# Rows of the maxima's matmuls in a projection stage, and three small operations moved from ScalarE to VectorE

## The chip, the cores and the metric

The kernel runs on one core of a Trainium2 chip. The metric is the device time of one execution in microseconds (us). The profile is that of one execution on the chip; its engines are PE (TensorE matmul), PEld (TensorE weight load), DVE (VectorE), ACT (ScalarE), POOL (GpSimd) and SP (SyncE, which here only issues DMAs).

## The reference

Both halves of the result read the same `x` (2048 rows of 448). `a` is a sliding, dilated local attention with 8 neighbours, `b` a full attention with 16 heads of 28 channels; a gate per row mixes the two.

```python
def _B_ref(x, wqkv, wo):
    B, S, D = x.shape              # 1, 2048, 448
    H = 16
    Dh = D // H                    # 28
    qkv = (lambda x, *d: x.transpose(*d))((x @ wqkv).reshape(B, S, 3, H, Dh), 2, 0, 3, 1, 4)
    q, k, v = qkv[0], qkv[1], qkv[2]
    scores = jnp.einsum("bhqd,bhkd->bhqk", q, k) * (Dh ** -0.5)
    p = _softmax(scores, axis=-1)
    o = jnp.einsum("bhqk,bhkd->bhqd", p, v)
    return (lambda x, *d: x.transpose(*d))(o, 0, 2, 1, 3).reshape(B, S, D) @ wo

x = A_x
g = _sigmoid((x * gate_w).sum(-1, keepdims=True))
a = _A_ref(x, A_wqkv, A_wo)        # 8 neighbours, 2 apart, own softmax
b = _B_ref(x, B_wqkv, B_wo)
return g * a + (1 - g) * b
```

## The kernel before, in words

The order of every engine is written out by hand: instructions run on each engine in the order in which the program issues them. There are three stages.

**Projections** (up to about 253 us of the profile). 92 tiles of `x @ w` are made, each a sum of products of a high and a low part of the operands (`ORDER`). The first ten tiles use all 128 rows of the array (`project`, 11 products). From tile 10 on, `project_halves` splits the contraction in two (11 products in one half, 10 in the other): half 0 uses rows 0 to 63 of the array, half 1 rows 64 to 127. Each half has a list (`todo[half]`), and the two lists are emitted in turn, one entry of each, so that neighbouring instructions use different halves and run beside each other; the two halves write the two banks of `PJ[n % 2]`. 28 tiles are of the kind "qk" (moving operand of 512 columns, line L303), the other 64 of the kinds "v" and "a" (448 or 450 columns, line L308).

Into 80 of these tiles, 11 to 90, work of the next stage is woven: the softmax of `b` needs the maximum of every row of the scores, and a first, rough product (28 channels, high parts alone) is made for it (`s1_mm`), four a tile, two PSUM tiles `PM[0]` and `PM[1]` of two banks each, and each `PM` is read by one VectorE maximum over 1024 columns (`TENSOR_REDUCE MX<-r`). One head has 28 channels at rows 32h to 32h+27. In the projections the product takes the whole half of 64 rows: the queries lie in two tiles, `QP[..][0]` for even heads and `QP[..][1]` for odd ones, and the rows of the other head of the half are zero. `s1_half(k, half)` is one such product; it is an entry of the half's list at index 2 (k = 0) and index 9 (k = 1), so both halves make one at the same place, and the second of the two issues the maximum.

**Attention** (`scores`, 253 to 827 us): 16 units (four groups of four heads, four blocks of 512 queries) of 16 steps. A step makes twelve products of 28 or 30 rows, four beside each other in the array, two exponentials on ScalarE, the products `av` with the values (`do_av`, 128 rows by 32 columns), and up to three more maxima's products, until all 1024 of them are made at step 235. At a unit's end `fin_copy` copies `av` out of its one PSUM bank, and `fin_hi` and others normalise and round it; hooks put each at a step. The last 21 steps have none.

**Output** (from 827 us): 16 tiles of the last projection.

Of the kernel before, what the change touches and what calls it, by code (L numbers as in the profile page):

```python
# [10 lines left out]
AF = mybir.ActivationFunctionType  # L11
ALU = mybir.AluOpType
X = mybir.AxisListType.X
ET = mybir.EngineType

S, D, H, DH = 2048, 448, 16, 28
# [4 lines left out]
NU = NG * NB  # L21
NMX = 192
# [3 lines left out]
def gated_mix_kernel(ctx: ExitStack, tc: tile.TileContext, xT, xn, gw, wA, wB, woAB, out):  # L26
    nc = tc.nc
# [25 lines left out]
    PJ, PM = PS[0:2], PS[2:4]  # L53
# [19 lines left out]
    MX = cp.tile([128, NMX], F32, name="MX")  # L73
# [13 lines left out]
    half = {}  # L87
# [10 lines left out]
    def dma_r(dst, src):  # L98
        nc.sync.dma_start(dst.bitcast(F32), src.bitcast(F32))
# [7 lines left out]
    def load_part(u, name, src):  # L107
        g, b = divmod(u, NB)
        t = sp.tile([128, 512], F32R, name=name)
        for h in range(4):  # L110
            r = 112 * g + DH * h
            dma_r(t[32 * h:32 * h + DH, :], src[r:r + DH, 512 * b:512 * b + 512])
        return t

    Qs = {}

    def load_q(u):
        Qs[u] = load_part(u, "QH", qk_hi), load_part(u, "QL", qk_lo)
        for i in range(2):
            dma_r(Qs[u][0][DH + i::32, :], nm[u][16 * i:16 * i + 16, :].rearrange("(h q) c -> h (q c)", h=4))  # L120

# [3 lines left out]
    s1c = [0]  # L125
    s1e = 64 * NU
    finished = []

    def load_qhi(u):
        g, b = divmod(u, NB)  # L130
        qhis[u] = QP[u % 2]
        for h in range(4):
            r = 112 * g + DH * h
            dma_r(qhis[u][h % 2][32 * h:32 * h + DH, :], qk_hi[r:r + DH, 512 * b:512 * b + 512])

    def s1_mm(n, bank, half=False):
        u, i = divmod(n, 64)
        qs, kc, h = i // 16, i // 4 % 4, i % 4
        if u == 0:
            qs, kc = i // 8 % 4, 2 * (i // 32) + i // 4 % 2  # L140
        if i == 0 and u + 1 < NU:
            load_qhi(u + 1)
        r = slice(64 * (h // 2), 64 * (h // 2) + 64) if half else slice(32 * h, 32 * h + DH)
        nc.tensor.matmul(bank, qhis[u][h % 2][r, 128 * qs:128 * qs + 128],  # L144
                         KH[u // NB % 3][r, 512 * kc:512 * kc + 512], start=True, stop=True)

# [9 lines left out]
        s1c[0] = n + k  # L156


    def s1_half(k, half):
        n = s1c[0]  # L160
        s1_mm(n + k + 2 * half, PM[k][:, half, :], True)
        halves[k] += 1
        if halves[k] == 2:
            halves[k] = 0
            m = MX[:, n % NMX:n % NMX + 4].rearrange("p (a b) -> p a b", b=2)[:, :, k]
            nc.vector.tensor_reduce(m, PM[k], axis=X, op=ALU.max)  # L166
            if k == 1:
                s1c[0] = n + 4
                if s1c[0] % 64 == 0:
                    finished.append(n // 64)  # L170

    halves = [0, 0]

# [18 lines left out]
    def max_turn(t):  # L194
        r = sp.tile([128, 32], F32, name="nms")
        nc.vector.transpose(r, t.bitcast(F32))
        return r
# [18 lines left out]
    with tc.tile_pool(name="xp", bufs=1) as xp, tc.tile_pool(name="wp", bufs=2) as wp:  # L216
# [99 lines left out]


        todo = [[], []]

        def project_halves(n, s1):  # L320
            if n % 2 == 0:
                for m in (n, n + 1):
                    low = (tiles[m][2] if tiles[m][1] == "qk" else tiles[m][-1] // 4) < 2
                    for half in range(2):
                        l = [p for p in ORDER if p != (0, 1, 3) or half == (0 if low else 1)]
                        l = [(m, product, (m, p, half, i == 0, i == len(l) - 1)) for i, p in enumerate(l)]
                        if s1[m - n]:
                            l[8:8] = [(m, s1_half, (1, half))]
                            l[2:2] = [(m, s1_half, (0, half))]
                        todo[half] += l  # L330
            while any(l and l[0][0] == n for l in todo):
                for l in todo:
                    if l:
                        _, f, x = l.pop(0)
                        f(*x)
# [83 lines left out]
        r, t = xst[:, 0, 0:3, :], xst[:, 0, 3, :]  # L419
# [5 lines left out]
        for kt in range(3):  # L425
            if kt < 2:
                nc.vector.tensor_copy(xh[0][:, kt, :], r[:, kt, :])
            nc.vector.tensor_tensor(out=xl[0][:, kt, :], in0=r[:, kt, :], in1=xh[0][:, kt, :].bitcast(F32),
                                    op=ALU.subtract)
        nc.vector.tensor_tensor(out=tail[64:128], in0=t[64:128], in1=tail[64:128].bitcast(F32), op=ALU.subtract)  # L430
        nc.vector.tensor_tensor(out=wl0[:, 3, 0:256], in0=wt0[:, 0:256], in1=wh0[:, 3, 0:256].bitcast(F32),
                                op=ALU.subtract)
# [27 lines left out]
        for n, t in enumerate(tiles):  # L460
# [4 lines left out]
            for w in splits:  # L465
                i, k = (n - splits[w][0]) * splits[w][1], splits[w][1]
# [36 lines left out]
            if parts and parts[0][0] <= n:  # L503
                _, u, t = parts.pop(0)
                max_store(u, max_turn(t))
            if finished and n < len(tiles) - 3:
                u = finished.pop(0)
# [12 lines left out]
            if n == 76:  # L520
                load_q(0)
# [5 lines left out]
    def at(pos, st, f):  # L527
        hooks.setdefault((st, pos), []).append(f)

    def run(pos, st):  # L530
        for f in hooks.pop((st, pos), ()):
            f()
# [8 lines left out]
    av = pool.tile([128, 512], F32, name="av")  # L541
# [33 lines left out]
    def mtile(name):  # L575
        return pm.tile([128, 512], F32, tag="M", name=name)
# [15 lines left out]
    for nme in ("k", "v"):  # L592
        for i in range(2):
            t = a1.tile([128, HALO + NJ, 56], F32, name=f"{nme}t{i}")
# [110 lines left out]
    for c in range(8):  # L705
# [20 lines left out]
        n = 0  # L726
# [17 lines left out]
    def issue(eng, st, limit):  # L744
        q = lists[eng]
        i = 0
        while i < min(len(q), LOOK):
            key, name, cost, needs, f = q[i]
            if any(d in names and issued.get(d, 10 ** 6) + lag > st for d, lag in needs):
                i += 1  # L750
                continue
            if eng in late:
                if late[eng] + cost > limit:
                    return
                late[eng] += cost
            f()
            issued[name] = st
            q.pop(i)
            i = 0
# [22 lines left out]
    def a_done(st):  # L782
        adone.append(st)
        assert st < OP0 + 24, st
        actx.close()
        oP["2"] = ctx.enter_context(tc.tile_pool(name="wop2", bufs=2))
        for k in range(4):
            at("end", max(st, OP0 + 23) + 2 * k, lambda k=k: (op_load_a(0, k), op_load_b(0, k)))
            at("dve", max(st, OP0 + 23) + 2 * k + 2, lambda k=k: op_split(0, k, nc.vector.tensor_copy))
# [61 lines left out]
    fin = {}  # L851
    def fin_copy(u):
        t = mp.tile([128, 512], F32, name="osb")
        nc.scalar.activation(t, av, AF.Copy)  # L854
        fin["o"] = t


# [26 lines left out]

    def fin_hi(u):
        fin["hi"] = mtile("onhi").bitcast(F32R)
        nc.scalar.activation(fin["hi"], fin["on"], AF.Copy)

    def fin_lo(u, eng):
        fin["lo"] = mtile("onlo").bitcast(F32R)  # L890
# [19 lines left out]
    for u in range(NU - 1):  # L910
        f = NJ * (u + 1)
        l = {NU - 3: (1, 2, 5, 6, 9, 12, 13, 15), NU - 2: (1, 2, 5, 6, 12, 15, 15, 15)}.get(
            u, (1, 3, 6, 8, 12, 15, 16, 19))
# [85 lines left out]
    for u in range(NU):  # L999
        g, b = divmod(u, NB)  # L1000
        for kt in range(NJ):
            st = NJ * u + kt
            now[0] = st
            if kt == 12 and u + 1 < NU:
                load_q(u + 1)
            run("pre", st)
            issue("sp", st, 0)
            if st >= A_START:
                issue("pool", st, 4.2)
            if not adone and not any(lists.values()) and st > stored[0]:  # L1010
                a_done(st)
            cur = {}
            left = s1e - s1c[0]
            for a in scores(u, kt, cur):
                if a == 2:
                    run("mid", st)
            run("dve", st)
            if u and kt == 6:
                late["dve"] += 0.25
            if finished:  # L1020
                v = finished.pop(0)
                t = max_parts(v, (lambda f: at("end", st + 1, f)) if v < NU - 1 else None)
                late["dve"] += 0.3
                turned = {}
                lag = 3 if v < NU - 1 else 1
                at("dve", st + lag, lambda t=t, w=turned: w.update(r=max_turn(t)))
                at("end", st + lag, lambda v=v, w=turned: max_store(v, w["r"]))
            issue("dve", st, DLIM)
            issue("act", st, 0)
            run("act", st)  # L1030
            if prev is not None:
                do_av(prev)
            else:
                nc.tensor.matmul(av[:, 0:384], ident, V[:, 0, 0:12, :].rearrange("p h e -> p (h e)"), start=True,  # L1034
                                 stop=True)
            prev = (kt, cur, g)
            if st == NJ * NU - 1:

                accs.extend((ring[0][:, 0, :], ring[1][:, 0, :]))
                op_mm(0, accs[0], (0, 1, 2), first=True)  # L1040
            run("end", st)
            step = 2.2 if left else 2.1
            late["dve"] = max(0.0, late["dve"] + 0.6 * min(3, left) - step)
            late["pool"] = max(0.0, late["pool"] - step)
    do_av(prev)
    fin_copy(15)

    u = NU - 1
# [30 lines left out]
```

## Time and profile before

| | |
|---|---|
| median of 3 runs | 901.83 us (901.52 to 901.9) |
| the profiled execution | 902.23 us, its span 900.5 us |
| PE busy | 893.1 us, 99% of the span |
| DVE, ACT, POOL busy | 737.6, 644.1, 640.5 us |
| granted clock | 0.999 |

The profiled execution lies 0.4 us above the median, and 1.7 us of it lie around the span. Line numbers (L144, L308) are those of the kernel before. A row of the timeline has the start, the length, the engine, the line, the operation, what it writes and reads, partitions x columns, and how many; a matmul's end is modelled, and its start tells more: the next one in the same rows starts well before this one's end.

### The profile page before, as it was taken

The page shows a single profiled execution, that of the slowest core. Times are in us where ns is not written, and L with a number is a line of the kernel's source. Part 1 is how long each engine was busy: PE and PEld are TensorE (multiplying, and loading weights), DVE is VectorE, ACT ScalarE, POOL GpSimd, SP SyncE. Part 2 cuts the span into 40 slices and gives each one's busy share as a digit, 9 for nine tenths or more (in the row PEclk, how much of TensorE's full clock was granted, in tenths as well). Part 3 has the DMA queues.
Part 4 walks back from the last instruction along what each step waited for, and adds up shares of the span by engine and source line. Part 5 has one row for each costly group of instructions (what it writes and reads, how often), then busy time and mean ns, then how long its engine had stood idle before and what let it go on. Part 6 is the DMA issues. An engine that isn't in the chain of part 4 may idle for free.

```text
span 900.5 us, 20546 instructions
## 1 busy us (share of the span) xinstructions
PE 893.1 (99%) x8326; PEld 527.6 (59%) x8326; DVE 737.6 (82%) x961; ACT 644.1 (72%) x770; POOL 640.5 (71%) x507
## 2 busy tenths in 40 slices
PE   8999999999999999999999999999999999999998
PEld 6888999999954434444444444444444444334997
DVE  5588999998979999999999999999999999821220
ACT  6456434343378888988988989889889899898220
POOL 2489846564459689999999999999999699501000
PEclk9999999999999999999999999999999999999999
DMA  9887503459473341226225342352220322245791
GB/s 257 289 263 197 157 12 84 134 133 106 114 249 73 94 131 48 71 50 161 71 55 143 86 114 62 90 139 63 56 63 19 90 43 56 75 102 158 216 286 54
DMA packets 116758, 105.04 MB, mean 117 GB/s; under 512 B 77192, under 2 KB 84744, under 8 KB 115880
## 3 DMA queue, kind: packets, MB, share of 16 engines
q1 hardware_dynamic: 116520, 103.47, 42.2%
q8 instruction: 65, 1.06, 0.5%
q10 hardware_dynamic: 144, 0.26, 0.1%
q14 instruction: 29, 0.24, 0.1%
HBM read 62.72 MB, written 40.96 MB: 115 GB/s over the span
## 4 chain that ended last, share of the span: by engine, by line
PE 97%; DMA 1%; ACT 1%; DVE 0%; SPq 0%; issue 0%; ACTq 0%
PE T L984 31%; PE av L950 28%; PE r L308 15%; PE T L836 8%; PE r L303 7%; PE r L144 4%; PE T L144 4%; DMA V<-in_xT 1%; ACT P L989 1%; DVE MX L166 0%; SPq L230 0%; ACT raw L371 0%; PE av L1034 0%; DVE xh L252 0%; ACT xh L250 0%
## 5 line engine op out<-in xcount | busy, mean ns | idle before, releaser
L989 ACT ACTIVATE P<-T 128x1024 f32<-128x1024 f32 x512 | 496.7, 1024 | 60.0 <-PE T L984 58.7
L150 DVE TENSOR_REDUCE MX<-T 128x1 f32<-128x512 f32 x470 | 442.2, 953 | 33.8 <-PE T L144 17.1
L950 PE MATMUL av<-P,V 128*32 128x512 f32 x2048 | 272.7, 605 | 0.4 <-ACT osb L854 0.4
L984 PEld LDWEIGHTS T<-QH,KH 30*128 30x128 f32 x1024 | 92.6, 181 | 230.6 <-ACT P L989 197.3
L144 PE MATMUL T<-KH,QP 28*128 28x512 f32 x704 | 220.2, 456 | 0.1
L984 PE MATMUL T<-QH,KH 30*128 30x512 f32 x1024 | 212.6, 489 | 0.2 <-ACT P L989 0.2
L166 DVE TENSOR_REDUCE MX<-r 128x2 f32<-128x1024 f32 x160 | 192.4, 1221 | 23.4 <-PE r L144 21.1
L984 PE MATMUL T<-QH,KL 28*128 28x512 f32 x1024 | 187.1, 395 | 0.0
L984 PE MATMUL T<-QL,KH 28*128 28x512 f32 x1024 | 184.9, 392 | 0.0
L613 POOL TENSOR_TENSOR prod<-qt,kt 128x896 f32<-128x896 f32 x64 | 135.4, 2116 | 5.1 <-DMA kt<-a_scr 5.1
L371 ACT ACTIVATE raw<-r 128x896 f32<-128x896 f32 (+1 forms) x64 | 58.9, 921 | 97.3 <-PE r L308 97.3
L144 PE MATMUL r<-KH,QP 64*128 64x512 f32 x320 | 105.2, 392 | 0.3 <-DVE MX L166 0.3
L674 POOL TENSOR_TENSOR oat<-oat,prod 128x896 f32<-128x896 f32 x48 | 101.2, 2109 | 2.0
L144 PEld LDWEIGHTS T<-KH,QP 28*128 28x128 f32 x704 | 86.0, 181 | 27.5 <-ACT P L989 18.6
L372 POOL TENSOR_TENSOR ast<-raw 128x448 f32<-128x448 f32 x48 | 55.4, 1154 | 58.5 <-ACT raw L371 48.2
L669 POOL TENSOR_TENSOR prod<-vt,L 128x896 f32<-128x896 f32 x56 | 95.3, 1702 | 0.2
L984 PEld LDWEIGHTS T<-QL,KH 28*128 28x128 f32 x1024 | 94.1, 184 | 0.0
L984 PEld LDWEIGHTS T<-QH,KL 28*128 28x128 f32 x1024 | 93.5, 183 | 0.6
L308 PE MATMUL r<-wh,xh 64*128 64x448 f32 (+1 forms) x512 | 93.2, 363 | 0.0
L950 PEld LDWEIGHTS av<-P,V 128*32 128x32 f32 x2048 | 40.3, 108 | 78.1 <-issue 65.3
L308 PEld LDWEIGHTS r<-wh,xh 64*128 64x128 f32 x512 | 74.1, 185 | 2.5
L308 PE MATMUL r<-wh,xl 64*128 64x448 f32 (+1 forms) x384 | 73.5, 364 | 0.0
(112 smaller groups left out, 1117.7 us busy)
## 6 DMA issues: line engine op xcount, KB each, us to landing
a_scr<-ast SPq DMA_DIRECT2D x24, 448.0 KB
qk_hi<-qkh SPq DMA_DIRECT2D x24, 256.0 KB
qk_lo<-qkh SPq DMA_DIRECT2D x24, 256.0 KB
rbc<-rs SPq DMA_DIRECT2D x64, 64.0 KB
QP<-qk_hi SPq DMA_DIRECT2D x64, 56.0 KB
KL<-qk_lo SPq DMA_DIRECT2D x16, 224.0 KB
QH<-qk_hi SPq DMA_DIRECT2D x64, 56.0 KB
QL<-qk_lo SPq DMA_DIRECT2D x64, 56.0 KB
```

The source lines that it names most:

```text
L144: nc.tensor.matmul(bank, qhis[u][h % 2][r, 128 * qs:128 * qs + 128], KH[u // NB % 3][r, 512 * kc:512 * kc + 512], start=True, stop=True)
L150: i = nc.vector.tensor_reduce(MX[:, n % NMX:n % NMX + k], bank, axis=X, op=ALU.max)
L166: nc.vector.tensor_reduce(m, PM[k], axis=X, op=ALU.max)
L303: nc.tensor.matmul(bank, ws[c][rows, k, t[4]:t[4] + 128], x, start=first, stop=last)
L308: nc.tensor.matmul(bank[:, 0:cols], x, ws[c][rows, k, 0:cols], start=first, stop=last)
L613: nc.gpsimd.tensor_tensor(out=p, in0=qt[c], in1=kvt["k", c % 2][:, HALO - DIL * w:HALO - DIL * w + NJ, :], op=ALU.mult)
L669: nc.gpsimd.tensor_tensor(out=dst.rearrange("p j (h d) -> p j h d", d=DH), in0=kvt["v", c % 2][:, HALO - DIL * w:HALO - DIL * w + NJ, :].r ...
L674: nc.gpsimd.tensor_tensor(out=ows[c % 2][:, :, 0:56] if w == W - 1 else oat[c], in0=oat[c], in1=oat[c, w], op=ALU.add)
L836: writes(bank, nc.tensor.matmul(bank[:, :D], src, wo[c][k], start=(first and k == ks[0] and i == 0), stop=(last and k == ks[-1] and i == 2)))
L950: nc.tensor.matmul(av[32 * h:32 * h + 32, :], V[:, kt, 4 * g + h, :], tiles_[h], start=(kt == 0), stop=(kt == NJ - 1), skip_group_check=True)
L984: nc.tensor.matmul(bank[a], (KH[g % 3], KH[g % 3], KL[g % 2])[t][r, ks], (qh, ql, qh)[t][r, :], start=(t == 0), stop=(t == 2))
L989: e = nc.scalar.activation(p, one if a == "2" else mine, AF.Exp, scale=SCALE).ins
```

## The change

In the projections the four maxima's products of a tile are no longer four entries of 64 rows but two entries of two products. The new `s1_pair(half)` issues both heads of one half behind each other, each on its own 28 rows, into the two banks of `PM[half]`, and then the maximum. Half 0 has its pair at index 2 of its list, half 1 at index 8. The number of maxima's products (320 in the projections), of maxima and their shapes stay.

In the last units three operations go from ScalarE to VectorE: the copy of the sums of unit 14 (`fin_copy`), and the rounding of units 13 and 14 (`fin_hi`). The query loads of the last unit are issued at step 9 of unit 14 instead of step 12; the rows with the maxima (`load_nm`) stay at step 12.

```diff
-    def s1_mm(n, bank, half=False):
+    def s1_mm(n, bank):
...
-        r = slice(64 * (h // 2), 64 * (h // 2) + 64) if half else slice(32 * h, 32 * h + DH)
+        r = slice(32 * h, 32 * h + DH)
         nc.tensor.matmul(bank, qhis[u][h % 2][r, 128 * qs:128 * qs + 128],
                          KH[u // NB % 3][r, 512 * kc:512 * kc + 512], start=True, stop=True)
...
-    def s1_half(k, half):
-        n = s1c[0]
-        s1_mm(n + k + 2 * half, PM[k][:, half, :], True)
-        halves[k] += 1
-        if halves[k] == 2:
-            halves[k] = 0
-            m = MX[:, n % NMX:n % NMX + 4].rearrange("p (a b) -> p a b", b=2)[:, :, k]
-            nc.vector.tensor_reduce(m, PM[k], axis=X, op=ALU.max)
-            if k == 1:
-                s1c[0] = n + 4
-                if s1c[0] % 64 == 0:
-                    finished.append(n // 64)
+    def s1_pair(half):
+        n = s1c[0] + 2 * half
+        for h in range(2):
+            s1_mm(n + h, PM[half][:, h, :])
+        nc.vector.tensor_reduce(MX[:, n % NMX:n % NMX + 2], PM[half], axis=X, op=ALU.max)
+        if half == 1:
+            s1c[0] = n + 2
+            if s1c[0] % 64 == 0:
+                finished.append(n // 64)
...
+        POS = 2, 8
...
-                            l[8:8] = [(m, s1_half, (1, half))]
-                            l[2:2] = [(m, s1_half, (0, half))]
+                            l[POS[half]:POS[half]] = [(m, s1_pair, (half,))]
...
     def fin_copy(u):
         t = mp.tile([128, 512], F32, name="osb")
-        nc.scalar.activation(t, av, AF.Copy)
+        if u == NU - 2:
+            nc.vector.tensor_copy(t, av)
+        else:
+            nc.scalar.activation(t, av, AF.Copy)
...
     def fin_hi(u):
         fin["hi"] = mtile("onhi").bitcast(F32R)
-        nc.scalar.activation(fin["hi"], fin["on"], AF.Copy)
+        if NU - 4 < u < NU - 1:
+            nc.vector.tensor_copy(fin["hi"], fin["on"])
+        else:
+            nc.scalar.activation(fin["hi"], fin["on"], AF.Copy)
...
-            if kt == 12 and u + 1 < NU:
+            if u + 2 < NU and kt == 12:
                 load_q(u + 1)
+            elif u + 2 == NU and kt == 9:
+                load_q(u + 1, False)
+            elif u + 2 == NU and kt == 12:
+                load_nm(u + 1)
```

On PE, one "v" or "a" tile of the projections (`r_132` is its `PJ`, `r_136` and `r_140` are `PM[0]` and `PM[1]`, `QP_157` and `QP_158` the queries of the even and the odd heads) stood like this before:

```order
L308 MATMUL r_132<-wh_1799,xh_182 128x448 x4
L144 MATMUL r_136<-KH_151,QP_157 128x512 x2
L308 MATMUL r_132<-wh_1799,xh_182 128x448 x4
L308 MATMUL r_132<-wl_1800,xh_182 128x448 x7
L308 MATMUL r_132<-wh_1799,xl_186 128x448
L144 MATMUL r_140<-KH_151,QP_158 128x512 x2
L308 MATMUL r_132<-wh_1799,xl_186 128x448 x5
```

After the change the same kind of tile stands like this:

```order
L308 MATMUL r_132<-wh_1799,xh_182 128x448 x5
L148 MATMUL r_136<-KH_151,QP_157 128x512
L148 MATMUL r_136<-KH_151,QP_158 128x512
L308 MATMUL r_132<-wh_1799,xh_182 128x448 x2
L308 MATMUL r_132<-wl_1800,xh_182 128x448
L308 MATMUL r_132<-wh_1799,xh_182 128x448
L308 MATMUL r_132<-wl_1800,xh_182 128x448 x6
L148 MATMUL r_140<-KH_151,QP_157 128x512
L148 MATMUL r_140<-KH_151,QP_158 128x512
L308 MATMUL r_132<-wh_1799,xl_186 128x448 x6
```

The counts are the same, 21 products and four for the maxima. Before, the two instructions of a place (x2) were one in each half, both of 64 rows; now they are the even and the odd head of one half, and the products of the other half stand ahead of and behind them.

On DVE, at the end of unit 13 and the start of the last unit (`tw` is a transpose of the local attention, `wor` the output weights that are split into `KH`, `KL` and `QP`), before:

```order
L680 STREAM_TRANSPOSE tw<-ow 128x256 x2
L779 CAST KH_152<-wor 128x448
L780 TENSOR_TENSOR KH_3279<-wor,KH_152 128x448
L680 STREAM_TRANSPOSE tw<-ow 128x256
...
L780 TENSOR_TENSOR KL_153<-wor,KH_152 128x448
L779 CAST KH_3279<-wor 128x448
L780 TENSOR_TENSOR KL_153<-wor,KH_3279 128x448
```

And after:

```order
L680 STREAM_TRANSPOSE tw<-ow 128x256
L891 CAST onhi<-on 128x512
L680 STREAM_TRANSPOSE tw<-ow 128x256
L779 CAST KH_152<-wor 128x448
L780 TENSOR_TENSOR KH_3279<-wor,KH_152 128x448
...
L780 TENSOR_TENSOR KL_153<-wor,KH_152 128x448
L855 COPY osb<-av 128x512
L779 CAST KH_3279<-wor 128x448
L780 TENSOR_TENSOR KL_153<-wor,KH_3279 128x448
```

The rounding of unit 13 (`onhi`) now stands between two transposes, and the copy of `av` behind the fourth split of the output weights and ahead of the fifth. ScalarE's queue has neither any more.

On SP, the loads ahead of the last unit, before:

```order
L775 DMA wor<-in_wo 128x448 x4
L201 DMA nm_115<-nms 32x32 x4
L99 DMA QH<-qk_hi 28x512 x4
L99 DMA QL<-qk_lo 28x512 x4
L99 DMA QH<-nm_115 4x512 x2
```

And after:

```order
L775 DMA wor<-in_wo 128x448
L99 DMA QH<-qk_hi 28x512 x4
L99 DMA QL<-qk_lo 28x512 x4
L775 DMA wor<-in_wo 128x448 x3
L201 DMA nm_115<-nms 32x32 x4
L99 DMA QH<-nm_115 4x512 x2
```

The eight query loads went ahead of three loads of output weights and of the four stores of the maxima.

More of the change, by code (lines that the diff above doesn't have):

```diff
@@ L115, in gated_mix_kernel, with load_q, load_nm @@
     Qs = {}
-    def load_q(u):
+    def load_q(u, low=True):
         Qs[u] = load_part(u, "QH", qk_hi), load_part(u, "QL", qk_lo)
+        if low:
+            load_nm(u)
+    def load_nm(u):
         for i in range(2):
@@ L156, in s1_max @@
         s1c[0] = n + k
-    def s1_half(k, half):
-        n = s1c[0]
-        s1_mm(n + k + 2 * half, PM[k][:, half, :], True)
-        halves[k] += 1
-        if halves[k] == 2:
-            halves[k] = 0
-            m = MX[:, n % NMX:n % NMX + 4].rearrange("p (a b) -> p a b", b=2)[:, :, k]
-            nc.vector.tensor_reduce(m, PM[k], axis=X, op=ALU.max)
-            if k == 1:
-                s1c[0] = n + 4
-                if s1c[0] % 64 == 0:
-                    finished.append(n // 64)
-    halves = [0, 0]
+    def s1_pair(half):
[7 more added lines that the diff above has]
+                finished.append(n // 64)
     def max_parts(u, later=None):
```

## The prediction

> **What bounds the kernel now.** I read the page first: how busy the engines are, and the chain of work that ended last.
>
> ```profile
> span 900.5 us, 20546 instructions
> PE 893.1 (99%) x8326; PEld 527.6 (59%) x8326; DVE 737.6 (82%) x961; ACT 644.1 (72%) x770; POOL 640.5 (71%) x507
> PE 97%; DMA 1%; ACT 1%; DVE 0%; SPq 0%; issue 0%; ACTq 0%
> PE T L984 31%; PE av L950 28%; PE r L308 15%; PE T L836 8%; PE r L303 7%; PE r L144 4%; PE T L144 4%; DMA V<-in_xT 1%; ACT P L989 1%; DVE MX L166 0%; SPq L230 0%; ACT raw L371 0%; PE av L1034 0%; DVE xh L252 0%; ACT xh L250 0%
> ```
>
> TensorE carries 97% of the chain, and the projections (the lines with `r`: L308, L303, L144) about a quarter of the span. Second, the windows of the two parts of that stage in which the maxima's products are woven in, the "qk" tiles and then the "v" and "a" tiles:
>
> ```profile
> core 0: us, PE busy (x) PEld busy (x) DVE busy (x) ACT busy (x) POOL busy (x), PEclk, DMA share, GB/s
> 36.50:89.10 52.60, 52.60 (x460) 45.80 (x458) 43.63 (x37) 30.10 (x45) 46.81 (x41) 1.00 0.79 244
> 89.10:250.90 161.80, 161.53 (x1543) 154.38 (x1541) 148.62 (x133) 64.58 (x84) 93.02 (x101) 1.00 0.46 105
> ```
>
> PE is busy throughout, at the full granted clock. VectorE stands close behind in the second window, 148.62 of 161.80 us. Third, the pieces of the chain by time and the group of the maxima's products give the time of a tile:
>
> ```profile
> 43.09 1.40 PE r L303 x12
> 48.89 1.40 PE r L303 x12
> ...
> 94.41 1.23 PE r L308 x12
> ...
> 99.65 1.23 PE r L308 x12
> ...
> L144 PE MATMUL r<-KH,QP 64*128 64x512 f32 x247 | 79.9, 393 | 0.3 <-DVE MX L166 0.3
> ```
>
> The pattern repeats every two tiles: 5.80 us for two "qk" tiles, so 2.90 each, and 5.24 us for two of the others, so 2.62 each. The last row agrees: 247 maxima's products, four a tile, are 61.75 tiles in 161.8 us, again 2.62. PE waited 0.3 us there in all. So this stage moves with PE's stream, and every 0.1 us on a tile is 8 us over the 80 tiles (17 "qk", 63 others).
>
> **Part 1: the pairs.** First the price of what is taken away. The timeline of the last tile, which has no maxima's products, gives the pitch of the others:
>
> ```profile
> 251.19 0.98 PE L308 MATMUL r<-wh,xh 64*128 64x448 f32 x8
> 252.01 0.78 PE L308 MATMUL r<-wl,xh 64*128 64x448 f32 x6
> ```
>
> Eight products, two beside each other, start in 0.82 us: 0.205 us a slot. A tile's 21 products take 10.5 slots, 2.15 us, so the four maxima's products take 2.62 - 2.15 = 0.47 us. In a "qk" tile 25 instructions take 2.90 us, 0.232 a slot, and the four take 0.46.
>
> In the new order the pair of 28-row products stands between 64-row products: into the pair and out of it, twice a tile, four changes a tile between 64-row and 32-row use of the array. Before had none within these tiles. What such a change costs is to be seen where the trace has one. From 64 to 30 rows at the end of the projections; from 128 to 64 at tile 10; from 28 to 128 in the first step of attention (PE rows, then the weight loads at the first):
>
> ```profile
> 253.25 0.36 PE L308 MATMUL r<-wh,xl 64*128 64x448 f32 x1
> 253.54 0.50 PE L984 MATMUL T<-QH,KH 30*128 30x512 f32 x2
> 253.88 0.39 PE L984 MATMUL T<-QL,KH 28*128 28x512 f32 x2
> ...
> 33.46 0.40 PE L303 MATMUL r<-xl,wh 128*128 128x512 f32 x1
> 33.79 0.73 PE L303 MATMUL r<-xh,wh 64*128 64x512 f32 x4
> ...
> 254.62 0.49 PE L144 MATMUL T<-KH,QP 28*128 28x512 f32 x2
> 255.05 0.59 PE L1034 MATMUL av<-V,ident 128*128 128x384 f32 x1
> ...
> 253.54 0.18 PEld L984 LDWEIGHTS T<-QH,KH 30*128 30x128 f32 x2 [0.31 <-issue]
> ```
>
> At the change the next product starts 0.29 us after the last one instead of 0.205 (0.33 instead of 0.23 at 512 columns). Its weights are not loaded ahead: the load starts with it, after 0.31 us in which none ran and no engine is named as its cause. So the first product is 0.11 us longer than the next (0.50 against 0.39), and its rows are free only after 0.34 us (253.54 to 253.88) instead of 0.23. If it is itself the last before a change, the next starts 0.43 us after it (254.62 to 255.05). A pair is just that case.
>
> One pair in a "v" or "a" tile then takes, from the last 64-row start ahead of it to the second one behind it: 0.29 in, 0.43 out, and 0.31 for the reloaded product behind it (0.34 less 0.03 for 448 instead of 512 columns), 1.03 us. Two slots of products in that stretch, 0.41 us, are there without the pair. The pair costs 0.62, two cost 1.24, against 0.47 now: 0.77 more a tile, 48.5 us over 63 tiles. In a "qk" tile: 0.33 + 0.43 + 0.34 - 0.46 = 0.64, twice 1.28 against 0.46: 0.82, 13.9 us over 17. Together 62.4 us.
>
> All of it lies on the path, since PE's order is fixed: a product of the other half that stands behind the pair can't start ahead of it. VectorE's load is the same, as many maxima of the same shape, and at 3.4 us a tile it has more time for them, so nothing new is late there.
>
> The Trainium skill has a rule that speaks against the change: "TensorEngine Tiling (Array Packing)", Key Properties, says that a change of the tiling mode, not of the tile alone, drains TensorE, and it lists 64 and 32 rows as different modes. The rows above agree for 128 to 64 and for 64 to 30, with 0.29 to 0.33 us from start to start; by the rule the four changes a tile are paid for as in my sum, without it none would be.
>
> What these rows don't show is a change in which the rows themselves are free: there the whole array went from one use to the other, while a pair takes half 0 and the next product half 1. The price of a change therefore lies between nothing and the 0.2 us of this sum, and I take the upper end, since all three rows show it and since the load ahead of time, which the rows in question would have allowed, was missing in each.
>
> **Part 2: the last units.** Here a step without maxima follows ScalarE. The timeline:
>
> ```profile
> 786.86 0.63 ACT L887 ACTIVATE onhi<-on 128x512 fp32r<-128x512 f32 x1
> 787.02 1.06 PE L950 MATMUL av<-P,V 128*32 128x512 f32 x8
> 789.37 1.06 PE L950 MATMUL av<-P,V 128*32 128x512 f32 x8
> ...
> 795.27 1.06 PE L950 MATMUL av<-P,V 128*32 128x512 f32 x8
> 797.19 0.60 ACT L854 ACTIVATE osb<-av 128x512 f32<-128x512 f32 x1
> 797.85 1.06 PE L950 MATMUL av<-P,V 128*32 128x512 f32 x8 [0.44 <-ACT osb L854]
> 799.74 1.06 PE L950 MATMUL av<-P,V 128*32 128x512 f32 x8
> 801.84 1.06 PE L950 MATMUL av<-P,V 128*32 128x512 f32 x8
> ...
> L845 DVE COPY res<-T 128x448 f32<-128x448 f32 x7 | 4.3, 620 | 38.2 <-PE T L836 16.7 <-ACT oahi L814 13.7 <-DMA onhi<-on_hi 7.8
> ```
>
> The undisturbed steps take 2.0 us on the mean (797.85 to 801.84 is two). The step with the rounding takes 2.35, the one with the copy 2.58. VectorE's copy out of PSUM takes 0.62 us for 448 columns, so 0.7 for 512; it can start when `av` ends at 795.27 + 1.06 = 796.33 and ends at 797.0, ahead of 795.27 + 2.0 = 797.27, where a step of 2.0 us would need it. So 0.35 and 0.58 go, 0.9 us; if a split of the output weights ahead of the copy makes VectorE late, half of that. The rounding of unit 14 falls in the last step, where PE has nine products of the output to make as well; I give it nothing. Behind the copy on VectorE three splits wait, by 0.7 us, for weights that are first used in the output stage, 30 us later; behind the rounding two transposes. On SP eight query loads overtake three loads of output weights and the stores of the maxima. The wait that the last unit's first steps show is for the copy and not for a load, so the earlier load brings nothing, and the delayed weights have the same 30 us. Part 2 is -0.9 us, between 0 and -1.2.
>
> **The sum.** The profiled execution took 902.23 us, of which 900.5 are the span; the median is 0.4 lower. 902.23 + 62.4 - 0.9 = 963.7, and 0.4 less is 963 us.
>
> **The rivals.**
>
> *Changes are cheaper (929 to 946).* The drain is paid and the reload is not, because the weights of rows that are free are loaded ahead: 0.29 in, 0.32 out (0.43 less 0.11), 0.205 behind: 0.82 - 0.41 = 0.41 a pair, 0.81 against 0.47, 0.34 a tile and 21.4 us; "qk" tiles 0.33 + 0.32 + 0.23 - 0.46 = 0.42, 0.38 a tile and 6.5 us. With part 2 and the median's 0.4 that is 929. Or the price stays and only the half with the pair is held, the other going one slot further at each of the two pairs of opposite halves, in sum one slot a tile: 80 times 0.21 us less than the forecast, 946. For it speaks that the rows above never had a free half; against it that the missing load ahead is the same in three different changes.
>
> *Changes cost nothing here (884): faster.* If 28-row and 64-row products in different rows run beside each other like two halves, a pair takes one slot of one half instead of one slot of both, and a tile loses 0.24 us: PE would need 2.15 + 0.23 = 2.38. VectorE then comes next: 148.62 us over 61.75 tiles is 2.41 us a tile. So 0.21 us over 63 tiles and 0.23 over 17 are 17 us, with part 2 18, and 884 us; PE's own bound would give 882. It decides from where four changes cost less than these 0.24 us, under 0.06 each; the cheapest part seen, the drain, is 0.29 - 0.205 = 0.085. What speaks for it is that the products of attention, 28 rows each and four beside each other, start within 0.01 us:
>
> ```profile
> 254.62 0.49 PE L984 MATMUL T<-QH,KL 28*128 28x512 f32 x2
> ```
>
> (these two beside the two L144 at the same 254.62). The Trainium skill, "TensorE: Matmul & The Clock Gate", Part 3, lets a weight load overlap a running product where the row groups differ; by that alone this rival would hold. No row here shows it across row counts.
>
> *The pair doesn't run side by side (998).* If the two products of a pair also follow each other, 0.205 to 0.23 us twice a tile come on top, 34 us. The row just shown speaks against it.
>
> **How the numbers follow.** The full price 0.47, the cheaper change 0.22, no price 0.27, the serial pair 0.03, and 0.01 that prices and gain cancel. A difference of 0.2%, 1.8 us, is what a measurement of this kernel can tell. Faster is 0.27, same 0.01, slower 0.72. The likeliest case has 946 to 972 as its own range. The range reaches over the cheaper changes to the faster case, 882, and to 972 above; it leaves out the serial pair and the tails, under 2 in 10.
>
> **What would show it.** In the changed kernel's timeline: the start of a pair 0.29 us after the last 64-row product, the next 64-row product 0.43 us after the pair, weight loads idle ahead of each; tiles of about 3.4 us, and VectorE's share of the second window down from 92% to about 71%. If instead pairs start 0.2 us after the last product with their weights loaded ahead and tiles take 2.4 us, the forecast is wrong in its price of a change. In the last units, steps of 2.0 us in place of 2.35 and 2.58.

## The result, and the profile after

The kernel after took 963.31 us (median of 4 runs, 963.08 to 963.85) against 901.87 us before (4 runs, 901.52 to 901.98): 1.0679 times as long, interval 1.0667 to 1.0692. The profiled execution took 963.08 us, its span is 961.3 us, 60.8 us more than before's 900.5. The top of the page, the chain of work that ended last and its groups:

```profile
span 961.3 us, 20549 instructions
PE 955.5 (99%) x8326; PEld 503.2 (52%) x8326; DVE 743.0 (77%) x964; ACT 642.4 (67%) x767; POOL 640.8 (67%) x507
...
PE 98%; ACT 1%; DMA 0%; SPq 0%; issue 0%; DVE 0%; ACTq 0%
PE T L990 29%; PE av L956 26%; PE r L308 17%; PE r L303 8%; PE r L148 7%; PE T L836 7%; PE T L148 4%; DMA raw<-in_wB 0%; ACT P L995 0%; SPq L230 0%; ACT raw L371 0%; PE av L1044 0%; ACT onhi L893 0%; ACT wh L224 0%; SPq L236 0%
```

TensorE makes the same 8326 matmuls and is the chain as before. Only the projections grew: the three lines with `r` were 26% of 900.5 us and are 32% of 961.3. The first product of attention starts at 315.2 us instead of 253.5, 61.7 later; from there to the first of the output it is 572.4 us instead of 573.3. Next the windows inside that stage ("qk" tiles, then "v" and "a" tiles), and the group of the maxima's products from 100 to 310 us:

```profile
36.50:98.00 61.50, 61.50 (x416) 36.60 (x418) 40.88 (x35) 27.93 (x43) 46.42 (x40) 1.00 0.65 199
100.00:310.00 210.00, 210.00 (x1546) 135.22 (x1542) 152.80 (x133) 63.42 (x84) 90.93 (x98) 1.00 0.34 80
```

```profile
L148 PE MATMUL r<-KH,QP 28*128 28x512 f32 x246 | 61.6, 495 | 0.0
```

246 products, four a tile, are 61.5 tiles in 210 us: 3.41 us a tile against 2.62 before. The clock stays at 1.00. PE counts as busy all the time, but its weight loads cover 64% of the second window instead of 95%, and VectorE 73% instead of 92%. The pieces of the chain, two tiles apart, give the same, first for "qk" tiles, then for the others:

```profile
62.61 1.60 PE r L303 x10
...
69.98 1.59 PE r L303 x11
...
147.15 1.42 PE r L308 x11
...
153.95 1.44 PE r L308 x11
```

7.37 us for two "qk" tiles is 3.69 each (2.90 before), 6.80 us for two others is 3.40. Within a tile the timeline shows one pair, first on PE, then on its weight loads:

```profile
151.09 0.78 PE L308 MATMUL r<-wl,xh 64*128 64x448 f32 x6
151.79 0.50 PE L148 MATMUL r<-KH,QP 28*128 28x512 f32 x2
152.22 0.47 PE L308 MATMUL r<-wh,xl 64*128 64x448 f32 x2
...
151.79 0.18 PEld L148 LDWEIGHTS r<-KH,QP 28*128 28x128 f32 x2 [0.30 <-issue]
152.22 0.30 PEld L308 LDWEIGHTS r<-wh,xl 64*128 64x128 f32 x4 [0.25 <-issue]
```

The six products start two beside each other, 0.205 us apart, the last two at 151.50. The pair starts at 151.79, 0.29 us after them; products of both halves start together at 152.22, 0.43 us after the pair; the next two follow at 152.53, 0.31 us on. Ahead of the pair and behind it no weights are loaded for 0.30 and 0.25 us. Over all 160 places of this trace the medians are the same, 0.295 in and 0.427 out.

The steps of the last units that the prediction named:

```profile
847.41 0.39 DVE L891 CAST onhi<-on 128x512 fp32r<-128x512 f32 x1
...
848.71 1.07 PE L956 MATMUL av<-P,V 128*32 128x512 f32 x8
850.61 1.06 PE L956 MATMUL av<-P,V 128*32 128x512 f32 x8
...
856.70 1.06 PE L956 MATMUL av<-P,V 128*32 128x512 f32 x8
858.67 1.06 PE L956 MATMUL av<-P,V 128*32 128x512 f32 x8
...
857.83 0.69 DVE L855 COPY osb<-av 128x512 f32<-128x512 f32 x1 [4.49 <-PE av L956]
```

The step with the rounding went from 2.35 to 1.90 us, the one with the copy from 2.58 to 1.97; the copy by VectorE takes 0.69 us.

### The profile page after: what moved, and what is told of

Same layout as the page of the kernel before. It is cut to its first block, busy times and chain, and to the rows that moved or that the text cites. A ratio compares the mean times of both kernels' runs of the same rounds, so it can differ in the third digit from the quotient of the medians.

```text
span 961.3 us, 20549 instructions
## 1 busy us (share of the span) xinstructions
PE 955.5 (99%) x8326; PEld 503.2 (52%) x8326; DVE 743.0 (77%) x964; ACT 642.4 (67%) x767; POOL 640.8 (67%) x507
## 4 chain that ended last, share of the span: by engine, by line
PE 98%; ACT 1%; DMA 0%; SPq 0%; issue 0%; DVE 0%; ACTq 0%
PE T L990 29%; PE av L956 26%; PE r L308 17%; PE r L303 8%; PE r L148 7%; PE T L836 7%; PE T L148 4%; DMA raw<-in_wB 0%; ACT P L995 0%; SPq L230 0%; ACT raw L371 0%; PE av L1044 0%; ACT onhi L893 0%; ACT wh L224 0%; SPq L236 0%
## 5 line engine op out<-in xcount | busy, mean ns | idle before, releaser
L167 DVE TENSOR_REDUCE MX<-r 128x2 f32<-128x1024 f32 x160 | 195.9, 1225 | 81.4 <-PE r L148 81.0
L308 PE MATMUL r<-wh,xh 64*128 64x448 f32 (+1 forms) x512 | 86.1, 389 | 0.0
L148 PE MATMUL r<-KH,QP 28*128 28x512 f32 x320 | 80.1, 495 | 0.0
L618 POOL TENSOR_TENSOR prod<-prod 128x448 f32<-128x448 f32 x64 | 65.6, 1026 | 5.0
L308 PE MATMUL r<-wh,xl 64*128 64x448 f32 (+1 forms) x384 | 67.7, 397 | 0.0
```

The costliest lines, as they stand in the source:

```text
L167: nc.vector.tensor_reduce(MX[:, n % NMX:n % NMX + 2], PM[half], axis=X, op=ALU.max)
L308: nc.tensor.matmul(bank[:, 0:cols], x, ws[c][rows, k, 0:cols], start=first, stop=last)
```

## The experiments

My theory: TensorE stops for every change between 64-row and 28-row products, the whole array with it, so the time goes by the number of changes and not by the number of 28-row products. The rivals: the new order costs the time, whatever the rows; each 28-row product costs a fixed amount; only the rows in question wait; or any row count other than 64 costs. Code is shown in part: `...` stands for lines left out, and the remarks behind # are not in the kernels. A ratio is that of a kernel's runs to runs of the kernel before in the same session, whose median lay between 902.55 and 903.08 us; behind it stands its 95% interval.

**The two parts apart.** *Tail alone:* the kernel before with only the edits of the change in `load_q` and its calls, `fin_copy` and `fin_hi`.

```diff
...
-        nc.scalar.activation(t, av, AF.Copy)
+        if u == NU - 2:
+            nc.vector.tensor_copy(t, av)
+        else:
+            nc.scalar.activation(t, av, AF.Copy)
...
```

> The part in the last units alone, on the kernel before; the projections are untouched. My theory: the two late steps (2.35 and 2.58 us) fall to 2.0 us, 0.9 us less, so about 901.0 us against 901.9. Rival (VectorE is late or the copy was not what the step waited for): within 0.3 us of before.

Measured: 901.7 us, 0.9988 of before (0.9979 to 0.9996): 0.9 us less by the medians (902.6 before), 1.1 by the ratio. *Pairs alone:* the kernel before with the rest of the change.

```diff
...
-                            l[8:8] = [(m, s1_half, (1, half))]
-                            l[2:2] = [(m, s1_half, (0, half))]
+                            l[POS[half]:POS[half]] = [(m, s1_pair, (half,))]
...
```

> The pairs of 28 rows alone, the last units as before. My theory (a change of the row count drains the array, four changes a tile): before + 62.4 us, 964 us, tiles of 3.39 us. Rival (part of the loss comes from the last units or from their interplay with the pairs): clearly below 963 us.

Measured: 964.34 us, 1.0685 (1.067 to 1.0699), 61.7 us more. The parts add up to the whole within these intervals.

**The rows or the order.** *The order of after, with 64 rows:* pairs, places and tail as after, each product again over the whole half.

```diff
...
-            s1_mm(n + h, PM[half][:, h, :])
+            s1_mm(n + h, PM[half][:, h, :], True)    # rows 64*(h//2) to 64*(h//2)+63
```

> The changed kernel in its order, but each product of a pair takes the 64 rows of its half again (the zeros of the other head are in the queries, so the result is the same). Only the rows differ from the changed kernel. My theory (the change of row count costs): no changes are left, so about the time before, 901 us, up to 918 if a slot of one half is lost at a pair whose two products now follow each other. Rival (the places, the order or the PSUM banks of the pair cost): near 963 us.

Measured: 901.11 us, 0.9982 (0.9973 to 0.9992). Its maxima's products from 110 to 240 us:

```profile
L148 PE MATMUL r<-KH,QP 64*128 64x512 f32 x196 | 61.3, 392 | 1.4 <-DVE MX L167 1.4
```

196 are 49 tiles in 130 us, 2.65 us each, as before. Between this kernel and after only the rows of these products differ, and all of the 61 us with them. *Before with 60 rows:*

```diff
-        r = slice(64 * (h // 2), 64 * (h // 2) + 64) if half else slice(32 * h, 32 * h + DH)
+        r = slice(64 * (h // 2), 64 * (h // 2) + 60) if half else slice(32 * h, 32 * h + DH)
```

> The kernel before with 60 rows instead of 64 in the maxima's products (rows 60 to 63 add nothing). My theory (what counts is which quarters of the array are used, not the exact number of rows): the same as before, 902 us. Rival (any other number of rows than the neighbours' is a change): four places without a common count, far slower, 960 us or more.

Measured: 901.78 us, 0.9992 (0.9982 to 1.0003): no difference. 60 rows among products of 64 are no change; 28 are.

**By the change or by the product.** *Four at one place:* all four 28-row products of a tile stand at index 2, so a tile has two changes instead of four.

```diff
...
-                            l[POS[half]:POS[half]] = [(m, s1_pair, (half,))]
+                            if half == 0:
+                                l[2:2] = [(m, s1_quad, ())]    # both pairs, then both maxima
+                            else:
+                                l[2:2] = [(m, nothing, ())]
```

> The changed kernel with its two pairs of a tile at one place, four 28-row products beside each other in all four quarters of the array, so two changes a tile instead of four. My theory (price by the change): one place costs 0.62 us against 0.47 for the four products before, 0.15 more in 63 tiles and 0.18 in 17, 12.5 us; 913 to 914 us. Rival (price by the 28-row product, 0.31 each): 963 us as with four changes.

Measured: 924.76 us, 1.0249 (1.0233 to 1.0264): by the number of products it would have stayed at 963. Over the kernel with 64 rows (901.11) the same 28-row products now cost 23.7 us instead of 62.2, but 11 more than I expected. *Four places of one product,* eight changes a tile:

```diff
...
-                            l[POS[half]:POS[half]] = [(m, s1_pair, (half,))]
+                            for k in (1, 0):               # POS = (1, 3), (7, 9)
+                                l[POS[half][k]:POS[half][k]] = [(m, s1_one, (half, k))]
```

> The changed kernel with the four 28-row products of a tile at four places, one each, so eight changes a tile. My theory (price by the change): four places at 0.62 us are 2.48 us a tile against 0.47, 2.01 more in 63 tiles and 2.1 in 17, 162 us, so about 1063 us. Rival (price by the 28-row product): 963 us.

Measured: 1078.84 us, 1.1958 (1.1938 to 1.1978), 16 us more than expected. Its group from 110 to 240 us, and the weight loads:

```profile
L148 PE MATMUL r<-KH,QP 28*128 28x512 f32 x107 | 52.9, 494 | 0.0
...
L148 PEld LDWEIGHTS r<-KH,QP 28*128 28x128 f32 x107 | 19.4, 181 | 33.9 <-issue 33.9
```

26.75 tiles in 130 us, 4.86 us each. On the mean each of these loads stands behind 0.32 us without any (33.9 us over 107), and nothing is named that they wait for. *The places of before, with 28 rows:* the kernel before; one product of each half stands at a place, two places a tile, as many changes as after.

```diff
-        s1_mm(n + k + 2 * half, PM[k][:, half, :], True)
+        s1_mm(n + k + 2 * half, PM[k][:, half, :])
```

> The kernel before in its own order (at each of two places one product in each half), with 28 rows instead of 64; the last units as before. My theory: two places, four changes a tile, the same as the pairs in one half, 964 us. Rival (two heads in one half, or their two banks of one tile, are what costs in the pair): near 902 us, or faster.

Measured: 974.11 us, 1.0794 (1.0778 to 1.081). Two products of different halves at a place cost about what the pair of one half costs; if two heads in one half or their two banks were the cost, it would be 902. So two, four and eight changes give 924.76, 963.31 (974.11 here) and 1078.84 us: the price goes by the change. What stayed open were the 10 to 16 us over my sums.

**What the sums lacked.** Of a tile's 21 products one half has 11, the other 10, in alternation, and the lists are emitted in turn. If a change holds both halves, then between two changes the half with fewer products stands idle for a slot of 0.2 us. After's places divide two tiles into stretches whose longer halves sum to 5 + 5 + 5 + 6 = 21 slots, no more than the 21 that 42 products need; in the kernel just shown it is 6 + 5 + 6 + 5 = 22. *That kernel with even stretches:* empty entries, and places moved by one in half 1, bring it to 21.

```diff
...
-                            l[8:8] = [(m, s1_half, (1, half))]
-                            l[2:2] = [(m, s1_half, (0, half))]
+                            gap, full = [(m, nothing, ())], len(l) == 11
+                            i, j = (3, 9) if half and full else (2, 8)
+                            l[j:j] = [(m, s1_half, (1, half))] + (gap if half and not full else [])
+                            l[i:i] = (gap if not half and not full else []) + [(m, s1_half, (0, half))]
```

> The kernel with one 28-row product in each half at two places of a tile (974 us), with the places of one half moved by one product and empty list entries, so that both halves have equally many products between two places (6, 5, 6, 4 slots in two tiles instead of 6, 5, 6, 5). The last units are as before. My theory (a half with one product less stands idle at a change): one slot in two tiles is saved, 0.10 us in 63 tiles and 0.115 in 17, 8.4 us, so 965.7 us. Rival (products of one head in each half are dearer than a pair in one half): 974 us.

Measured: 966.13 us, 1.07 (1.0682 to 1.0718), 8 us less than with 22 slots; 40 times 0.205 us is 8.2. The forecast held and the rival fell. Four places of one product come to 23 slots by the same count, two too many, 16.4 us: about as much as that kernel lay above its forecast, though no even version of it was run.

*Four at one place, evened out:* the empty entry of half 1 goes to index 3 of its list where that has 11 products, so that its stretches take 21 slots instead of 22.

```diff
-                                l[2:2] = [(m, nothing, ())]
+                                i = 2 if len(l) == 10 else 3
+                                l[i:i] = [(m, nothing, ())]
```

> The four 28-row products at one place as in the quad, but the place is moved by one product in every second tile, so that between two places both halves have equally many products (11 and 11, 10 and 10) instead of 11 and 10. What my sum left out: a change waits for both halves, so a half with one product less stands idle for a slot. My theory: one slot in two tiles is saved, 0.10 us in 63 tiles and 0.115 in 17, 8.4 us against the quad, 916 us. Rival (the 11 us by which the quad was over its forecast come from the maxima, which all start at one place, or from a dearer change): 924 to 925 us.

Measured: 923.48 us, 1.0224 (1.0207 to 1.0241): 1.3 us won by the medians and 2.3 by the ratios, not 8. The timeline of a place in every second tile, first on PE, then the maxima on VectorE:

```profile
152.58 0.59 PE L322 MATMUL r<-wh,xh 64*128 64x450 f32 x4
153.10 0.75 PE L148 MATMUL r<-KH,QP 28*128 28x512 f32 x4
153.78 0.69 PE L322 MATMUL r<-wh,xh 64*128 64x450 f32 x4
...
150.94 2.35 DVE L169 TENSOR_REDUCE MX<-r 128x2 f32<-128x1024 f32 x2 [0.78 <-PE r L148]
```

The first two of the four start at 153.10, the other two only 0.25 us later, at 153.35: they write `PM[1]`, whose maximum of the tile before ends on VectorE at 153.29. With both maxima of a tile issued at once, an earlier place meets VectorE. Over the 80 places of this trace the last of the four starts 9.6 us after the first in sum, against 3.3 us in the kernel with 22 slots. So 6.3 of the 8.2 us came back as a wait. In the kernel with 22 slots the lost slots (8.2 us) and its own wait (3.3) together are 11.5 us, the 11 that it lay above its forecast.

**Whether the free half waits too.** *A half almost free:* half 0 keeps one product a tile, and both pairs stand there among twelve empty entries, always with heads 0 and 1. Left out are the rest of half 0's products (nine or ten a tile) and the maxima of heads 2 and 3.

```diff
...
+                            if half == 0:
+                                l = [(m, product, (m, l[0][2][1], half, True, True))] + 12 * gap
+                                for k in range(2):
+                                    l[POS[k]] = (m, s1_pair, (k,))
+                            l += (13 - len(l)) * gap       # gap: one empty entry
```

> Half 0 makes one product a tile and then only the two pairs, always in the rows of heads 0 and 1; half 1 makes its products as in the changed kernel. It leaves out ten products of half 0 in each of these tiles and the maxima of heads 2 and 3. The rows of a pair are free when it is issued, and those of the product behind it too. My theory (a change of the row count drains the whole array): a pair still starts 0.29 us after the last product of half 1 and holds the next one for 0.43 us; tiles of 10.5 slots and two pairs at 0.62, about 3.4 us. Rival (only a conflict in the same rows costs): pairs run beside half 1, tiles of 2.15 us by PE, 2.4 by VectorE.

Measured, one run: 1165.44 us. The granted clock was 1.00 in the first of these tiles and 0.50 later. The two windows, the pairs in the first (tiles of the kind "qk"), then the group of the maxima's products and a pair in the second:

```profile
36.50:48.70 12.20, 12.20 (x54) 7.09 (x52) 7.39 (x7) 5.06 (x7) 6.33 (x5) 1.00 0.87 295
110.00:240.00 130.00, 130.00 (x335) 78.95 (x333) 53.32 (x46) 27.67 (x40) 41.76 (x38) 0.50 0.18 51
...
36.68 0.50 PE L149 MATMUL r<-KH,QP 28*128 28x512 f32 x2
37.11 0.96 PE L307 MATMUL r<-xh,wh 64*128 64x512 f32 x3
37.91 0.85 PE L307 MATMUL r<-xh,wl 64*128 64x512 f32 x3
38.69 0.50 PE L149 MATMUL r<-KH,QP 28*128 28x512 f32 x2
39.13 0.50 PE L307 MATMUL r<-xh,wl 64*128 64x512 f32 x1
39.14 0.50 PE L307 MATMUL r<-xh,wh 64*128 64x512 f32 x1
...
44.31 0.49 PE L149 MATMUL r<-KH,QP 28*128 28x512 f32 x2
...
L149 PE MATMUL r<-KH,QP 28*128 28x512 f32 x88 | 35.0, 790 | 0.0
...
200.05 1.32 PE L312 MATMUL r<-wl,xh 64*128 64x448 f32 x3
201.17 0.57 PE L312 MATMUL r<-wh,xl 64*128 64x448 f32 x1
201.67 0.80 PE L149 MATMUL r<-KH,QP 28*128 28x512 f32 x2
202.40 0.74 PE L312 MATMUL r<-wh,xl 64*128 64x448 f32 x1
202.41 0.74 PE L312 MATMUL r<-wh,xh 64*128 64x448 f32 x1
```

At the full clock first. Between the pairs at 36.68 and 38.69 half 1 makes six products one after another and half 0 none, so the second pair's rows have nothing to do. Still it starts 0.31 us after the last of the six (at 38.38), and products of both halves start together 0.43 to 0.45 us after it, close to the 0.33 and 0.43 that the prediction took for a "qk" tile. From 36.68 to 44.31 are two tiles, 3.8 us each, where 10.5 slots of 0.232 and two pairs at 0.64 are 3.7. The rival, tiles of 2.4 us with the pair beside the other half, falls. At the clock of 0.50 the same is to be seen, stretched: 0.50 us in, 0.73 out, half 1's products 0.37 apart (200.05 to 201.17 in three steps) instead of 0.205, each 1.7 to 1.8 times as long, and 22 tiles in 130 us, 5.9 us each. *The same with 64 rows* for the maxima's products (the same is left out):

```diff
-        r = slice(32 * h, 32 * h + DH)
+        r = slice(0, 64) if low else slice(32 * h, 32 * h + DH)    # low: called from s1_pair
```

> The kernel with half 0 nearly empty again, with the maxima's products in all 64 rows of half 0, so that no row count changes; it leaves out the same products of half 0 and the maxima of heads 2 and 3. It asks why the granted clock was 0.5 in the projections there. If the changes of the row count did it: clock 1.0 and tiles of 2.4 us, VectorE's bound. If a half-empty array did it: clock about 0.5 and tiles well over 2.4 us, near 4 (10.5 slots of 0.37).

Measured, one run: 878.83 us. The window, its group and the timeline:

```profile
110.00:240.00 130.00, 128.87 (x910) 105.41 (x909) 126.81 (x122) 61.38 (x79) 75.86 (x93) 1.00 0.55 123
...
L149 PE MATMUL r<-KH,QP 64*128 64x512 f32 x206 | 74.8, 443 | 0.2
...
151.10 0.49 PE L149 MATMUL r<-KH,QP 64*128 64x512 f32 x1
151.11 0.37 PE L312 MATMUL r<-wl,xh 64*128 64x450 f32 x1
```

With equal rows a maximum's product runs beside half 1, a tile takes 2.52 us (51.5 in 130 us) and VectorE, busy 126.81 of 130 us, sets it. So the whole array stops for a change, also where the rows in question are free.

*Two empty entries ahead of half 0's pair* were to show the same in the kernel after:

```diff
...
+                            if half == 0:
+                                l[2:2] = 2 * [(m, nothing, ())]
+                            else:
+                                l += 2 * [(m, nothing, ())]
```

> The changed kernel with two empty entries in the list of half 0 ahead of its pair (and two at the end of half 1's), so that the rows of the pair have been free for two slots, about 0.4 us, when it is issued, with half 1 at work in them. Nothing is left out. My theory (a change drains the whole array): the pair of half 0 still starts 0.29 us after the last product of half 1, and the product of half 1 behind it, whose rows are free too, 0.43 us after the pair; tiles of 3.40 us and up to 0.4 for the empty entries. Rival (a conflict in the same rows): the pair starts with or right behind the last product of half 1 and tiles get shorter by 0.3 us or more.

Measured, one run: 964.55 us, tiles as after. It decides nothing on this point, for a reason I had not expected: the empty entries cost no slot, because a half runs ahead of the other. They only move products: the stretches become 7 + 3 + 7 + 4 slots in two tiles, again 21, with both halves at work in each. The timeline:

```profile
153.91 0.36 PE L311 MATMUL r<-wh,xh 64*128 64x450 f32 x1
153.91 0.56 PE L311 MATMUL r<-wh,xl 64*128 64x448 f32 x2
154.11 0.37 PE L311 MATMUL r<-wh,xh 64*128 64x450 f32 x1
```

The products with 450 columns belong to the next tile. In the program all `wh,xl` products of the tile with 448 columns stand ahead of them; yet one of the next tile starts at 153.91, 0.2 us before the last `wh,xl` of the old tile (the second of the x2, at 154.11), in the other half.

## Why the prediction was right

The forecast was 963.0 us with 0.47 for its case; the median is 963.31. The total is closer than its largest term, the pairs, which cost 61.7 us and not 62.4; that part of the agreement is luck.

**The price of a change.** The three starts came out as worked from the rows of other stages: 0.29 in, 0.43 out, 0.31 for the reloaded product. A tile grew by 0.78 us against 0.77 forecast ("v" and "a", 2.62 to 3.40), a "qk" tile by 0.79 against 0.82. The choice that decided was to take the upper end for rows that are free; the prediction had no row for it, and the almost free half shows why it holds: the stop is that of the whole array. The rule of the Trainium skill, "TensorEngine Tiling (Array Packing)", Key Properties, that a change of the mode drains TensorE, agrees with every run here: 64 rows in the same order cost nothing (0.9982), and the price follows the number of changes.

**The rivals.** Cheaper changes (929 to 946) and changes for nothing (884) needed either weights loaded ahead or one half going on. Neither is in the trace: the loads stand still for 0.25 to 0.30 us at each change, and both halves start together behind a pair. The serial pair did not happen: both products of a pair start at 151.79. (Its 998 should be 997, 34 more than 963; nothing hangs on it.)

**"PE's order is fixed".** The conclusion, that all of the price lies on the path, was right; the reason was not right in general. A product can start ahead of one of the other half that stands before it (0.2 us in the last timeline). What holds both halves behind a pair is the change.

**What the sum left out.** It counted two slots against each pair and took for granted that both halves are equally long between changes. After's places happen to divide the products so that no slot is lost (21 of 21), which was luck. With other places, as in the kernel with before's places, the same sum missed by 10 us; 8 of these are shown by the even version.

**VectorE** fell to 73% of the window (forecast about 71%) and nothing new was late there.

**The last units.** Forecast -0.9 us; measured -0.9 by the medians of the tail alone, -1.1 by its ratio (-0.4 to -1.9 by its interval), and -0.9 between the first product of attention and the first of the output in after. The two steps became 0.45 and 0.61 us shorter where 0.35 and 0.58 were forecast. Which of the three operations and the earlier load brought how much was not run apart.

**What beats both.** The tail alone (0.9988) and the order of after with 64 rows (0.9982) are both slightly faster than before, by 0.9 to 1.6 us; their intervals overlap, so which is better stays open. Both keep what the change did in the last units, and neither has a change of the row count in the projections.

## What to carry to other kernels

Before cutting a matmul's rows to pack more of them beside each other, count the switches between row counts in the order in which they are issued, not the products. In this kernel a place where one or two 28-row products stand among 64-row ones cost 0.62 us, three slots, and there were two such places, while the four 64-row products that they replaced took 0.47 us together. If a narrow product has to stand there, put as many as possible at one place, give both halves the same work between places, and check that the buffers which they fill at once are free.

## What the runs showed of the hardware that I had not expected

**Halves overtake each other.** A product started 0.2 us before one of the other half that stands ahead of it in the program. The Trainium skill, "TensorE: Matmul & The Clock Gate", Part 3, says that matmuls start and end in program order; the timeline of the kernel with two empty entries differs, and the measurement decides.

**A clock of 0.50 while PE counts as busy.** The kernel with one half almost free and 28-row pairs had a granted clock of 1.00 in the first 12 us of these tiles, then 0.50 in the projections, 0.799 on the mean, with PE busy 130.00 of 130.00 us. The same with 64 rows had 1.00, and after, with as many changes a tile but both halves at work, 1.00 too. So neither the half-empty array nor the changes alone lower it; together they did in one run. The Trainium skill, "TensorE: Matmul & The Clock Gate", Part 1, lets the clock follow how busy TensorE has lately been; for that to agree, the stops would have to count as idle there though the profile shows them as busy. No run here tells that apart, and the cause stays open.
